# Half-row steps in the MLP phase of a spectral adaLN block's forward and backward pass

## The chip, the cores and the metric

The kernel runs on one core of a Trainium2 chip. The metric is device time in microseconds of one execution. Before the change the median of three runs is 533.21 us (532.02 to 536.06). Engines are named as in the profile: PE multiplies matrices (PEld loads its weights), DVE and ACT work on rows in SBUF and PSUM, SP issues the DMAs, POOL is hardly used here.

## The reference

S = 2048 rows, D = 512, F = 1792; all inputs are bf16. `c` and `w_mod` give six modulation rows, of which `gb`, `cb` and `ga` matter here. The outputs are the result of this block and its gradients for every input.

```
def A(x, w_r, w_i):                      # spectral filter
    X = rfft2(x) * (w_r + 1j * w_i)
    return irfft2(X)
def B(x, w1, b1, w2, b2):                # MLP, squared relu
    r = relu(x @ w1 + b1)
    return (r * r) @ w2 + b2
sa, ca, ga, sb, cb, gb = (silu(c) @ w_mod).reshape(6, D)
x1  = x  + ga * A(layernorm(x) * (1 + ca) + sa)
out = x1 + gb * B(layernorm(x1) * (1 + cb) + sb)
grads = vjp(out)(grad_out)
```

## The kernel before

The Fourier transforms are matmuls with constant matrices. The rows stand in 16 tiles of 128 rows, and the MLP phase takes them in four blocks of four tiles (512 rows); F is cut into 14 slices of 128. A number in brackets is the block.

Ahead of the MLP phase, PE computes gaT = (grad_out * 2gb) @ w2T, transposed, for all blocks: 224 matmuls of 512 columns (L601), that are given a late priority, so that they fill the gaps of the spectral stages. The MLP phase then has these stages for block b:

- `stage_g`: the last two spectral steps of each row tile (psT, L332, to Tsb on ACT; psY, L339, to y on ACT), then x1 and its layernorm on DVE, which gives n2rows.
- `stage_t`: 16 PE transposes of n2rows (L711) into h2T, evacuated by DVE and ACT in turn.
- `stage_h`: 14 slices of h (L732), relu on ACT (r, L733), then on DVE gh = r * gaT in place (L735) and h = r * r (L737); both are also written to DRAM.
- `stage_o`: for each row tile one matmul of b2 (L792) and 14 of h and w2 (L794), then out0 and gp = gb * o on DVE.
- `stage_gn`: for each row tile 14 matmuls of gh and w1T (L766), then on ACT and DVE cb, jk and the gradient row gx1, which is written to DRAM. For blocks 2 and 3 the first backward spectral step of that row (`spec_f1_row`, L232 to L239) follows late.
- `colsums` (L661): column sums on PE, delayed by two row tiles.

w1T is loaded by a transposing DMA after the last gaT matmul has freed its place, behind w2 and ahead of b2row on SP. It is then scaled by 1 + cb (L673) and has a mean added (L674, nmean). nmean comes from 56 one-column matmuls of w1 and the row 1 + cb (L668).

The first backward spectral step of the rows of blocks 0 and 1 (eight row tiles) needs the place UT that is only free in block 2; their gradient rows are loaded again from DRAM in pairs (L825), multiplied by ga on DVE (L826) and taken by PE in one block between `stage_h(2)` and `stage_o(2)`.

The program is written in stages in Python, but a scheduler with priorities sets the order on each engine: it takes an instruction that is ready, by its own costs, in the order of the program. Every engine then works in order. Tiles of a pool have a given number of buffers (`bufs`), and a new tile waits for the last use of the one it takes the place of.

Of the kernel before, what the change touches and what calls it, by code (L numbers as in the profile page):

```python
# [10 lines left out]
ALU = mybir.AluOpType  # L11
# [313 lines left out]
def spec_g23(tc, K, CS, t, tpool, psT_pool, psY_pool):  # L325

    nc = tc.nc
    ps = psT_pool.tile([P, D], FP32, name="psT")
# [7 lines left out]
    psY = psY_pool.tile([P, D], FP32, name="psY")  # L336
# [3 lines left out]
    return psY  # L340

# [65 lines left out]
def kernel(  # L407
# [174 lines left out]
    cb1b = constp.tile([P, 4], BF16, name="cb1b")  # L582
    nc.vector.tensor_copy(cb1b, mcol[:, CB1_C])
# [70 lines left out]
    with tc.tile_pool(name="psR", bufs=1, space=PSUM) as psR, tc.tile_pool(name="psO", bufs=2, space=PSUM) as psO_pool, \  # L654
# [10 lines left out]
        psr = psR.tile([P, NFC], FP32, name="pst2")  # L665
        for fc in range(NFC):
            for dc in range(4):
                nc.tensor.matmul(psr[:, fc:fc + 1], lhsT=w1[:, dc, fc * P:(fc + 1) * P], rhs=cb1b[:, dc:dc + 1],  # L668
                                 start=(dc == 0), stop=(dc == 3))
        nmean = wp.tile([P, NFC], FP32, name="nmean")  # L670
        nc.vector.tensor_scalar(nmean, psr, -1.0 / D, None, op0=ALU.mult)
        for fc in range(NFC):
            nc.vector.tensor_tensor(w1T[:, fc, :], w1T[:, fc, :], modb[:, CB1_B, :], op=ALU.mult)  # L673
            nc.vector.tensor_scalar(w1T[:, fc, :], w1T[:, fc, :], nmean[:, fc:fc + 1], None, op0=ALU.add)  # L674
# [4 lines left out]

        def stage_g(b):  # L680
            n2b[b] = rows.tile([P, TB, D], BF16, name="n2rows")
            x1b[b] = rows.tile([P, TB, D], BF16, name="x1")
            yb[b] = rows.tile([P, TB, D], BF16, name="y")
            nc.sync.dma_start(x1b[b], x_view[:, TB * b:TB * b + TB, :])
            for j in range(0, TB, 2):
                t = TB * b + j
                x1, y = x1b[b][:, j:j + 2, :], yb[b][:, j:j + 2, :]
                for i in range(2):
                    psY = spec_g23(tc, K, CS, t + i, rows, psR, psR)
                    nc.scalar.copy(out=y[:, i, :], in_=psY)  # L690
# [11 lines left out]
            nc.sync.dma_start(n2_dram[:, TB * b:TB * b + TB, :], n2b[b])  # L702

        def stage_t(b):
            n2rows = n2b[b]
            hb = rows.tile([P, 4, SB], BF16, name="h2T")
            h2T[b] = hb
            for dc in range(4):
                pst = psR.tile([P, TB, P], BF16, name="pst2")
                for j in range(TB):  # L710
                    nc.tensor.transpose(pst[:, j, :], n2rows[:, j, dc * P:(dc + 1) * P], K["ident"])  # L711
                src = pst.rearrange("p j q -> p (j q)")
                if dc % 2 == 0:
                    nc.vector.tensor_scalar(hb[:, dc, :], src, mcol[:, CB1_C, dc:dc + 1], mcol[:, SB_C, dc:dc + 1], op0=ALU.mult, op1=ALU.add)
# [399 lines left out]
```

## Time and profile before

| what | before |
|---|---|
| median of three runs | 533.21 us |
| the profiled execution | 533.43 us |
| its span | 531.6 us |
| granted PE clock, mean | 0.957 |
| PE busy | 450.7 us (85%) |
| DVE busy | 358.0 us (67%) |
| ACT busy | 239.7 us (45%) |

All times in the tables of stretches count from the start of the span. Ahead of 91 us lie the forward spectral steps, from 91 to 139 us the rest of gaT with the first two blocks' last spectral steps, from 139 to 335 us the four blocks of the MLP phase, and behind it the weight gradients and the rest of the backward spectral steps. In a timeline a row's start and length are given, and in square brackets how long its engine sat idle before it and which instruction ended that. Matmuls are pipelined, so that the lengths of neighbouring groups overlap; the distance of two starts is the better measure of what a group costs.

### The profile page before, as it was taken

The page shows a single profiled execution, that of the slowest core. Times are in us where ns is not written, and L with a number is a line of the kernel's source. Part 1 is how long each engine was busy: PE and PEld are TensorE (multiplying, and loading weights), DVE is VectorE, ACT ScalarE, POOL GpSimd, SP SyncE. Part 2 cuts the span into 40 slices and gives each one's busy share as a digit, 9 for nine tenths or more (in the row PEclk, how much of TensorE's full clock was granted, in tenths as well). Part 3 has the DMA queues.
Part 4 walks back from the last instruction along what each step waited for, and adds up shares of the span by engine and source line. Part 5 has one row for each costly group of instructions (what it writes and reads, how often), then busy time and mean ns, then how long its engine had stood idle before and what let it go on. Part 6 is the DMA issues. An engine that isn't in the chain of part 4 may idle for free.

```text
span 531.6 us, 7352 instructions
## 1 busy us (share of the span) xinstructions
PE 450.7 (85%) x2527; PEld 226.8 (43%) x2563; DVE 358.0 (67%) x849; ACT 239.7 (45%) x415; POOL 12.4 (2%) x56
## 2 busy tenths in 40 slices
PE   0868998899898999979599999866985999869995
PEld 0434465554343444434344434443442465424442
DVE  5878998294386670496647745267787667459976
ACT  3456865473453161345342722562312247626524
POOL 4111000000000000000000000000000000000000
PEclk9969999899999999999989999997899799979999
DMA  8954879420493298199511979575556619988997
GB/s 282 217 161 99 333 211 292 173 81 39 146 302 127 79 251 184 41 213 309 170 59 44 266 225 197 158 249 145 118 150 220 154 53 276 212 241 242 271 248 242
DMA packets 148062, 99.40 MB, mean 187 GB/s; under 512 B 93362, under 2 KB 134840, under 8 KB 147384
## 3 DMA queue, kind: packets, MB, share of 16 engines
q1 hardware_dynamic: 148024, 98.93, 68.0%
q8 instruction: 20, 0.33, 0.3%
q14 instruction: 18, 0.15, 0.1%
HBM read 37.26 MB, written 39.61 MB: 145 GB/s over the span
## 4 chain that ended last, share of the span: by engine, by line
PE 49%; DMA 17%; DVE 16%; SPq 11%; issue 3%; ACT 3%; DVEq 0%; ACTq 0%
PE og L794 9%; PE mm L732 7%; PE og L766 6%; PE mm L601 6%; PE mm L972 5%; PE mm L895 4%; SPq L494 3%; DMA w1T<-in_B_w_dram 3%; SPq L471 3%; DMA w1s<-in_B_w_dram 3%; PE psG L301 2%; PE psY L339 2%; PE psT L332 2%; DMA n_sb<-n_dram 2%; DMA gb<-in_grad_out_dram 2%
## 5 line engine op out<-in xcount | busy, mean ns | idle before, releaser
L895 PE MATMUL mm<-gab,n_sb 128*128 128x448 bf16 x256 | 56.0, 380 | 5.4 <-DVE gjk L903 5.4
L601 PE MATMUL mm<-gT,w2T 128*128 128x512 bf16 x213 | 53.8, 384 | 3.4 <-DVE gab L604 1.9
L732 PE MATMUL mm<-h2T,w 128*128 128x512 bf16 x219 | 52.9, 378 | 1.7 <-ACT h2T L716 0.9
L794 PE MATMUL og<-w,h 128*128 128x512 bf16 x218 | 52.0, 381 | 2.7 <-DVE h L737 2.4
L972 PE MATMUL mm<-g_sb,hn 128*128 128x512 bf16 x217 | 51.4, 384 | 0.5 <-issue 0.3
L766 PE MATMUL og<-w1T,gab 128*128 128x512 bf16 x218 | 49.7, 379 | 0.3
L733 ACT ACTIVATE r<-mm,b1col 128x512 bf16<-128x512 f32 x56 | 38.1, 687 | 20.1 <-PE mm L732 10.7
L895 PEld LDWEIGHTS <-n_sb 128*128 128x128 bf16 x256 | 26.5, 104 | 34.9 <-issue 15.7
L732 PEld LDWEIGHTS <-w 128*128 128x128 bf16 x224 | 21.3, 97 | 29.1 <-issue 7.9
L794 PEld LDWEIGHTS <-h 128*128 128x128 bf16 x224 | 20.7, 98 | 28.4 <-DVE h L737 3.9
L766 PEld LDWEIGHTS <-gab 128*128 128x128 bf16 x224 | 21.7, 98 | 26.0 <-issue 0.8
L601 PEld LDWEIGHTS <-w2T 128*128 128x128 bf16 x224 | 21.7, 98 | 25.9 <-issue 6.2
L972 PEld LDWEIGHTS <-hn 128*128 128x128 bf16 x224 | 21.2, 98 | 26.1 <-issue 3.8
L604 DVE CAST gab<-mm 128x512 bf16<-128x512 f32 x28 | 19.2, 687 | 18.5 <-PE mm L601 13.8
L770 DVE SCALAR_TENSOR_TENSOR jk<-cb,onef,n2rows 128x512 bf16<-128x512 bf16 x16 | 12.0, 749 | 27.8 <-ACT cb L767 27.8
L735 DVE TENSOR_TENSOR gab<-r,gab 128x1024 bf16<-128x1024 bf16 x28 | 19.3, 690 | 10.4 <-ACT r L733 10.4
L767 ACT ACTIVATE cb<-og,inv 128x512 bf16<-128x512 f32 x16 | 11.0, 688 | 33.4 <-PE og L766 33.4
L606 ACT CAST gab<-mm 128x512 bf16<-128x512 f32 x28 | 16.4, 587 | 20.7 <-PE mm L601 20.6
L335 ACT ACTIVATE Tsb<-psT 128x512 bf16<-128x512 f32 x32 | 18.3, 598 | 14.7 <-PE psT L332 14.6
L901 DVE SCALAR_TENSOR_TENSOR gw<-mm,mcol,gtmp 128x448 bf16<-128x448 f32 x16 | 10.9, 682 | 18.5 <-PE mm L895 17.5
L795 ACT CAST o<-og 128x512 bf16<-128x512 f32 x16 | 9.2, 588 | 30.4 <-PE og L794 27.5
L339 PE MATMUL psY<-Tsb,TAT 128*128 128x256 bf16 x128 | 18.8, 277 | 1.8 <-ACT y L690 1.5
(272 smaller groups left out, 791.4 us busy)
## 6 DMA issues: line engine op xcount, KB each, us to landing
gh_dram<-gab SPq DMA_DIRECT2D x28, 256.0 KB, 3.3
h_dram<-h SPq DMA_DIRECT2D x28, 256.0 KB, 3.1
w<-in_B_w_dram SPq DMA_DIRECT2D x2, 1792.0 KB, 8.0
wm<-in_w_mod_dram SPq DMA_DIRECT2D x3, 1024.0 KB, 8.2
wmc<-in_w_mod_dram SPq DMA_DIRECT2D x12, 256.0 KB
out_dram<-gwm SPq DMA_DIRECT2D x12, 256.0 KB, 3.9
xs_dram<-Xs SPq DMA_DIRECT2D x8, 258.0 KB, 3.3
Xb<-xs_dram SPq DMA_DIRECT2D x8, 258.0 KB, 3.0
```

Of the source, the lines that this page charges most:

```text
L335: nc.scalar.activation(Tsb, ps, AF.Copy, scale=EF_S)
L339: nc.tensor.matmul(psY[:, H * s:H * s + H], lhsT=K["TAT"][:, s * e], rhs=Tsb[:, H * e:H * e + H], start=(e == 0), stop=(e == 1))
L601: nc.tensor.matmul(ps, lhsT=w2T[:, dc, fc * P:(fc + 1) * P], rhs=gT[b][:, dc, :], start=(dc == 0), stop=(dc == 3))
L604: nc.vector.tensor_copy(out=gaT[b][:, fc, :], in_=ps)
L606: nc.scalar.copy(out=gaT[b][:, fc, :], in_=ps)
L732: nc.tensor.matmul(ps, lhsT=w1[:, dc, (fc + i) * P:(fc + i + 1) * P], rhs=h2T[b][:, dc, :], start=(dc == 0), stop=(dc == 3))
L733: nc.scalar.activation(r[:, i, :], ps, AF.Relu, bias=b1col[:, fc + i:fc + i + 1])
L735: nc.vector.tensor_tensor(gh, r, gh, op=ALU.mult)
L766: nc.tensor.matmul(ps, lhsT=gaT[b][:, fc, (j + i) * P:(j + i + 1) * P], rhs=w1T[:, fc, :], start=(fc == 0), stop=(fc == NFC - 1))
L794: nc.tensor.matmul(ps, lhsT=hT[b, fc][:, (j + i) * P:(j + i + 1) * P], rhs=w2[:, fc, :], start=False, stop=(fc == NFC - 1))
L895: nc.tensor.matmul(ps[:, 0:W4], lhsT=n2_sb[:, t, dc * P:(dc + 1) * P], rhs=ghn[t // 4][:, t % 4, fs], start=(t == 0), stop=(t == NT - 1))
L972: nc.tensor.matmul(ps, lhsT=hns[fc][:, t, :], rhs=g_sb[:, t, :], start=(t == 0), stop=(t == NT - 1))
```

## The change

Four things change.

(a) The 56 matmuls of L668 are gone. w1T is scaled by a SCALAR_TENSOR_TENSOR that also sums its row into nmean (L687 after); after all 14, nmean is scaled (L689) and added (L691).

(b) The stages return lists of steps, and `merge` deals them between each other: the steps of `stage_g(b+1)` and the transposing DMAs of the gh of block b-1 between the half rows (seven matmuls) of `stage_o(b)`, the transposes of `stage_t(b+1)` between the half rows of `stage_gn(b)`. The eight reloaded rows (`f1_again`, L865 and L866) go from the block ahead of `stage_o(2)` to between the half rows of `stage_gn(3)`. Their place is a buffer of `gx1` (two, shared with the gradient rows), no longer of `o`.

(c) x1 and grad_out rows (gb) are loaded by `load_rows` at the start of `stage_h` one block ahead, gb with two buffers instead of one; h2T has one buffer instead of two.

(d) In `stage_h`, h is computed and written ahead of gh.

```
-            for dc in range(4):
-                nc.tensor.matmul(psr[:, fc:fc + 1], lhsT=w1[:, dc, fc * P:(fc + 1) * P], rhs=cb1b[:, dc:dc + 1],
-                                 start=(dc == 0), stop=(dc == 3))
-        nc.vector.tensor_scalar(nmean, psr, -1.0 / D, None, op0=ALU.mult)
+            nc.vector.scalar_tensor_tensor(out=w1T[:, fc, :], in0=w1T[:, fc, :], scalar=K["onef"], in1=modb[:, CB1_B, :], op0=ALU.mult, op1=ALU.mult,
+                                           accum_out=nmean[:, fc:fc + 1])
+        nc.vector.tensor_scalar(nmean, nmean, -1.0 / D, None, op0=ALU.mult)
         for fc in range(NFC):
-            nc.vector.tensor_tensor(w1T[:, fc, :], w1T[:, fc, :], modb[:, CB1_B, :], op=ALU.mult)
             nc.vector.tensor_scalar(w1T[:, fc, :], w1T[:, fc, :], nmean[:, fc:fc + 1], None, op0=ALU.add)
...
+def merge(main, *fills):
+    fill = [f for fl in fills for f in fl]
+    k = 0
+    for i, m in enumerate(main):
+        m()
+        while k < len(fill) and k * len(main) < (i + 1) * len(fill):
+            fill[k]()
+            k += 1
...
+        def load_rows(b):
+            if b < NB:
+                x1b[b] = rows.tile([P, TB, D], BF16, name="x1")
+                nc.sync.dma_start(x1b[b], x_view[:, TB * b:TB * b + TB, :])
+            if b > 0:
+                gbt[b - 1] = rows.tile([P, TB, D], BF16, name="gb")
+                nc.sync.dma_start(gbt[b - 1], g_view[:, TB * (b - 1):TB * b, :])
...
+        def f1_again(UT):
+            gxl = {}
+            def one(t):
+                if t % 2 == 0:
+                    gxl[0] = rows.tile([P, 2, D], BF16, name="gx1")
+                    nc.sync.dma_start(gxl[0], gx1_dram[:, t:t + 2, :])
+                    nc.vector.tensor_tensor(gxl[0], gxl[0], modb[:, GA_B, None, :].broadcast_to([P, 2, D]), op=ALU.mult)
+                spec_f1_row(tc, K, gxl[0][:, t % 2, :], t, UT, psR, ("psT", "psY")[t % 2])
+            return [lambda t=t: one(t) for t in range(2 * TB)]
...
+        for b in range(NB):
+            stage_h(b)
+            parts = [lambda fc=fc: ghn_part(b - 1, fc) for fc in range(0, NFC, 2)] if b > 0 else []
+            if b < NB - 1:
+                merge(stage_o(b), [x for p in zip(stage_g(b + 1), parts + [lambda: None] * 8) for x in p])
+                if b == NB - 2:
+                    UT = utcs.tile([P, 4, 16, NT, 8], BF16, name="utcs")
+                merge(stage_gn(b, UT), [lambda: None] * 2 + stage_t(b + 1))
+            else:
...
+                merge(stage_gn(b, UT), [x for p in zip(f1_again(UT), parts + [lambda: None]) for x in p])
+                merge(stage_o(b))
```

What stands on an engine is decided by the scheduler, so three places follow as the two programs have them. The first is DVE at the end of `stage_h(0)`, where w1T is prepared. Before (the last rows of the preparation, six more pairs of L673 and L674 stand ahead):

```order
L673 TENSOR_TENSOR w1T<-w1T,modb 128x512 x2
L674 TENSOR_SCALAR w1T<-w1T,nmean 128x512 x2
L737 TENSOR_TENSOR h<-r 128x1024
L735 TENSOR_TENSOR gab<-r,gab 128x1024
L737 TENSOR_TENSOR h<-r 128x1024
L714 TENSOR_SCALAR h2T<-pst_1908,mcol 128x512
L735 TENSOR_TENSOR gab<-r,gab 128x1024
L737 TENSOR_TENSOR h<-r 128x1024
```

The same place after the change (gab is gh, L773 is h, L847 belongs to `stage_o(0)`):

```order
L773 TENSOR_TENSOR h<-r 128x1024
L777 TENSOR_TENSOR gab<-r,gab 128x1024
L749 TENSOR_SCALAR h2T<-pst_1950,mcol 128x512
L773 TENSOR_TENSOR h<-r 128x1024
L687 SCALAR_TENSOR_TENSOR w1T,nmean<-w1T,onef,modb 128x512 x14
L777 TENSOR_TENSOR gab<-r,gab 128x1024
L689 TENSOR_SCALAR nmean<-nmean 128x14
L847 TENSOR_TENSOR gp<-gb,o 128x1024
L691 TENSOR_SCALAR w1T<-w1T,nmean 128x512 x14
```

All h of the block now stand ahead of the preparation, whose two passes are apart. On PE, the 16 transposes of block 0, and four of block 1, have moved from between the first matmuls of `stage_h(0)` to among the last gaT matmuls.

The second place is ACT from the end of `stage_h(2)` to `stage_o(2)`. Before (r is of `stage_h`, y and Tsb of the spectral steps of block 3, utcs of the reloaded rows, o of `stage_o`):

```order
L733 ACTIVATE r<-mm,b1col 128x512 x14
L690 CAST y<-psY 128x512 x2
L335 ACTIVATE Tsb<-psT 128x512
L690 CAST y<-psY 128x512 x2
L239 CAST utcs<-psY 128x64x8
L239 CAST utcs<-psT 128x64x8
L349 ACTIVATE inv_70<-l_mv,eps 128x2
L239 CAST utcs<-psY 128x64x8
L349 ACTIVATE inv_70<-l_mv,eps 128x2
L239 CAST utcs<-psY 128x64x8
L795 CAST o<-og 128x512 x2
```

After:

```order
L771 ACTIVATE r<-mm,b1col 128x512 x2
L717 CAST y<-psY 128x512
L335 ACTIVATE Tsb<-psT 128x512
L771 ACTIVATE r<-mm,b1col 128x512 x8
L371 ACTIVATE inv_70<-l_mv,eps 128x2
L771 ACTIVATE r<-mm,b1col 128x512 x4
L842 CAST o<-og 128x512 x3
L717 CAST y<-psY 128x512
L842 CAST o<-og 128x512
L717 CAST y<-psY 128x512
L806 ACTIVATE cb<-og,inv_70 128x512
```

The spectral steps of block 3 now stand within `stage_h(2)` and `stage_o(2)`, and the reloaded rows are no longer there; PE has the transposes of block 3 between the rows of `stage_gn(2)`, where before they stood in and behind that block. The same steps of block 2 stand where they stood, within and behind `stage_gn(1)`.

The third place is DVE in `stage_gn(3)`. Before:

```order
L770 SCALAR_TENSOR_TENSOR jk,rb<-cb,onef,n2rows 128x512
L771 TENSOR_SCALAR rb<-rb 128x1
L770 SCALAR_TENSOR_TENSOR jk,rb<-cb,onef,n2rows 128x512
L771 TENSOR_SCALAR rb<-rb 128x1
L772 SCALAR_TENSOR_TENSOR gx_3199<-n2rows,rb,gb 128x512 x2
L770 SCALAR_TENSOR_TENSOR jk,rb<-cb,onef,n2rows 128x512
```

After (L866 is the multiply of a reloaded pair):

```order
L811 SCALAR_TENSOR_TENSOR gx_3072<-n2rows,rb,gb 128x512
L866 TENSOR_TENSOR gx_3121<-gx_3121,modb 128x1024
L809 SCALAR_TENSOR_TENSOR jk,rb<-cb,onef,n2rows 128x512
L810 TENSOR_SCALAR rb<-rb 128x1
L811 SCALAR_TENSOR_TENSOR gx_3072<-n2rows,rb,gb 128x512
L815 TENSOR_TENSOR gx_3072<-gx_3072,cb 128x1024
L818 TENSOR_TENSOR cb<-gx_3072,modb 128x1024
L820 TENSOR_TENSOR y<-gx_3072,y 128x1024
L866 TENSOR_TENSOR gx_3171<-gx_3171,modb 128x1024
L809 SCALAR_TENSOR_TENSOR jk,rb<-cb,onef,n2rows 128x512
```

The multiplies of three reloaded pairs stand among the rows of `stage_gn(3)`. All four reloads take the same buffer of gx1 one after the other, so that the DMA of each waits for the matmuls of the pair before it.

More of the change, by code (lines that the diff above doesn't have):

```diff
@@ L335, in spec_g23, with spec_g3 @@
     nc.scalar.activation(Tsb, ps, AF.Copy, scale=EF_S)
[L336 removed]
+    return Tsb
+def spec_g3(tc, K, Tsb, pool):
+    nc = tc.nc
+    psY = pool.tile([P, D], FP32, name="psY")
+    H = D // 2
     for s in range(2):
```

165 lines of the change are left out of this document (78 added, 87 removed).

## The prediction

> **What bounds the kernel now.** I read the page first: the busy shares, and the shares of the chain that ended last.
>
> ```profile
> PE 450.7 (85%) x2527; PEld 226.8 (43%) x2563; DVE 358.0 (67%) x849; ACT 239.7 (45%) x415; POOL 12.4 (2%) x56
> PE 49%; DMA 17%; DVE 16%; SPq 11%; issue 3%; ACT 3%; DVEq 0%; ACTq 0%
> ```
>
> PE is busy for 85% of the span but makes only 49% of the chain, so a good part of the time goes through work that PE waits for. To find where, I cut the MLP phase into stretches. The columns are the stretch, its length, the busy time and instructions of PE, PEld, DVE, ACT and POOL, the granted PE clock, the DMA share and GB/s.
>
> ```profile
> 97.00:139.00 42.00, 40.36 (x212) 21.32 (x215) 25.29 (x53) 21.69 (x40) 0.00 (x0) 0.96 0.16 55
> 139.00:187.00 48.00, 42.91 (x213) 18.92 (x217) 30.03 (x67) 18.54 (x28) 0.00 (x0) 1.00 0.61 181
> 187.00:237.00 50.00, 46.12 (x231) 20.82 (x235) 29.14 (x62) 21.34 (x36) 0.00 (x0) 1.00 0.70 172
> 237.00:291.00 54.00, 47.39 (x240) 22.75 (x242) 34.23 (x67) 22.13 (x38) 0.00 (x0) 0.94 0.48 153
> 291.00:335.00 44.00, 42.68 (x208) 18.92 (x210) 25.09 (x47) 17.54 (x28) 0.14 (x2) 1.00 0.87 210
> ```
>
> PE is the bound in all of them: in the second to fifth row it lacks 5.1, 3.9, 6.6 and 1.3 us of busy time. Two rows stand out: 139 to 187 (block 0) and 237 to 291 (block 2), the latter also with a clock of 0.94. These, and the one matmul group that the change removes, I read in the timeline of PE (start, length, line, instruction, idle time before it and its releaser). First the removed group:
>
> ```profile
> 95.45 1.57 PE L668 MATMUL pst<-cb1b,w 128*128 128x1 bf16 x56 [3.66 <-DMA w<-in_B_w_dram]
> ```
>
> Then block 0, from the last gaT matmul to the first h of block 1:
>
> ```profile
> 133.69 5.28 PE L601 MATMUL mm<-gT,w2T 128*128 128x512 bf16 x22
> 139.24 0.38 PE L711 MATMUL pst<-ident,n2rows 128*128 128x128 bf16 x4 [0.26 <-DVE nmean L671]
> 140.26 0.38 PE L711 MATMUL pst<-ident,n2rows 128*128 128x128 bf16 x4 [0.64 <-DVE h2T L714]
> 140.48 0.59 PE L732 MATMUL mm<-h2T,w 128*128 128x512 bf16 x2
> ...
> 148.59 7.43 PE L732 MATMUL mm<-h2T,w 128*128 128x512 bf16 x32 [0.18 <-ACT r L733]
> 155.85 0.39 PE L711 MATMUL pst<-ident,n2rows 128*128 128x128 bf16 x4
> ...
> 163.12 1.04 PE L794 MATMUL og<-w,h 128*128 128x512 bf16 x4 [2.36 <-DVE h L737]
> ...
> 170.83 0.38 PE L792 MATMUL og<-b2row,ones_sq 1*128 1x512 bf16 x1
> ...
> 174.18 12.25 PE L766 MATMUL og<-w1T,gab 128*128 128x512 bf16 x55
> ...
> 186.91 1.47 PE L732 MATMUL mm<-h2T,w 128*128 128x512 bf16 x6
> ```
>
> PE runs dry at the first transposes, and later for 2.36 us at the last slices of h. gaT ends at 133.69 + 5.28 = 138.97, which I call E, and block 1 starts at 186.91 = E + 47.9. Then block 2, between its h and its rows of h*w2, where the spectral steps of block 3 (L339), the reloaded rows (L232, operand o) and the transposes (L711) stand in a row:
>
> ```profile
> 255.36 0.60 PE L339 MATMUL psY<-Tsb,TAT 128*128 128x256 bf16 x4 [0.68 <-ACT y L690]
> ...
> 259.93 0.27 PE L232 MATMUL psT<-TA,o 128*128 128x256 bf16 x1 [1.43 <-DVE utcs L237]
> ...
> 263.55 0.61 PE L711 MATMUL pst<-ident,n2rows 128*128 128x128 bf16 x2 [1.43 <-DVE n2rows L701]
> 265.13 0.39 PE L232 MATMUL psT<-TA,o 128*128 128x256 bf16 x1 [0.97 <-DVE o L826]
> ...
> 268.96 0.60 PE L792 MATMUL og<-b2row,ones_sq 1*128 1x512 bf16 x1
> ...
> 291.10 3.11 PE L732 MATMUL mm<-h2T,w 128*128 128x512 bf16 x13
> ```
>
> Each step here waits for another engine, and nothing else is queued on PE that could go ahead. The same stretch as a window:
>
> ```profile
> 254.69:268.96 14.27, 8.27 (x48) 5.22 (x49) 11.20 (x26) 6.90 (x14) 0.00 (x0) 0.82 0.35 116
> ```
>
> PE is busy 8.27 of 14.27 us, and at a clock of 0.82, though no single wait is over 1.43 us.
>
> **Part 1, up to the end of gaT.** L668 waited 3.66 us for the load of w1 and took 1.57 us; gaT matmuls, which wait for nothing there, take its place: -5.2. The 20 transposes that now stand among the gaT matmuls cost PE (from the start of 140.26 to that of 140.48, four in 0.22) 20 x 0.055 = +1.1, and leave the next part. Sum -4.1. Bounds: -5.2 if they fit into waits that are there, and -2.2 if n2rows, which DVE makes just before, comes late for two waits like the one of 0.97 at 265.13.
>
> **Part 2, from E to block 1.** Here I build the time forward, since the waits change places. 32 matmuls of h go from 148.59 to 155.85, 0.227 each, so 56 end at E + 12.7, as the transposes are done by then and, with all h ahead of w1T on DVE, the wait of 2.36 is gone. What is late next is a DMA: `stage_o(0)` begins with b2row. SP's rows, and the transposing load from the chain of waits:
>
> ```profile
> 139.44 12.54 SPq L646 DMA_TRANSPOSE w1T<-in_B_w_dram  x1
> 152.03 0.42 SPq L648 DMA_DIRECT2D b2row<-in_B_b_dram  x1
> ```
>
> ```profile
> 139.44 14.54 DMA w1T<-in_B_w_dram
> ```
>
> SP is held for 12.54 us by the issue of w1T and gives out b2row at 152.03. Its landing has no row of its own; the nearest is that of the DRAM tile of gradient rows, for 256 KB:
>
> ```profile
> DMA to landing us min/median/max: 2.1/3.7/5.7
> ```
>
> I take its least, 2.1 us, for 1 KB: 154.1 or E + 15.2, a new wait of 2.5 us. SP waits for the same gaT matmul before and after, so this moves with E. A row of h*w2 takes 174.18 - 170.83 = 3.35, four 13.4: E + 28.6. Then `stage_gn(0)`, by the row at 174.18 12.2 us, the 12 transposes left 0.7 and the column sums 186.91 - 186.43 = 0.5, gives block 1 at E + 42.0 if w1T is ready. That is decided on DVE:
>
> ```profile
> L770 DVE SCALAR_TENSOR_TENSOR jk<-cb,onef,n2rows 128x512 bf16<-128x512 bf16 x16 | 12.0, 749 | 27.8 <-ACT cb L767 27.8
> ```
>
> ```profile
> L673 DVE TENSOR_TENSOR w1T<-w1T,modb 128x512 bf16<-128x512 bf16 x14 | 5.3, 422 | 0.2 <-DMA w1T<-in_B_w_dram 0.2
> L674 DVE TENSOR_SCALAR w1T<-w1T,nmean 128x512 bf16<-128x512 bf16 x14 | 4.3, 351 | 0.0
> ```
>
> w1T lands at 139.44 + 14.54 = E + 15.0. The old scaling took 0.42 an instruction, or 5.3 us for all; the new one I price by jk, the same operation with a sum in the same shape, 0.749: 14 make 10.5, E + 25.5. Three instructions stand between, at most 0.75 each, so the additions begin by E + 27.7 and end 4.3 us later, E + 32.0. The first is needed at 28.6, the last at 28.6 + 13/14 of a row of 3.05 = 31.4: +0.6. Block 1 starts at E + 42.6, against 47.9: **-5.3**. gab of the last pair now waits behind the 14 scalings, but is needed in `stage_gn(0)` alone, as late as those. Bounds: -5.9 with w1T in time, and -1.7 with b2row at the largest landing, 5.7.
>
> **Part 3, blocks 1 and 2 up to the h of block 3.** For block 2's spectral steps the order is unchanged, so `stage_gn(1)` and what follows stay as they are: 0. The earlier loads of x1 and gb take waits from DVE that PE does not see there: 0. In block 2 the row of 14.27 us breaks up. What stays on PE are 16 matmuls of psY at 0.109 (half of one of 512 columns) and four transposes, 1.9 in all, now between rows; 12.4 go. Of the waits I let one stay, the 1.43 for n2rows: the second pair's layernorm is still made on DVE while `stage_gn(2)` starts, and the transposes stand in order ahead of its later rows. **-11.0**. Bounds: -12.4 without this wait, and -3.5 if every wait comes back in the new place and only the reloaded rows leave.
>
> **Part 4, block 3.** The eight reloaded rows come back here. Two rows of this kind, when nothing waits, take
>
> ```profile
> 295.26:296.14 0.88, 0.88 (x10) 0.78 (x9) 0.88 (x2) 0.57 (x2) 0.00 (x0) 1.00 1.30 250
> ```
>
> 0.88 us, four pairs 3.5. Their loads are no longer hidden: each waits for the previous pair's matmuls, since they share one buffer. The first load is issued in `stage_gn(2)` and is in time. Between pairs PE has, by the order, 18 matmuls and six column sums (4.4 us at 0.217, 12.2/56), then 15 (3.3), then 17 and four of 256 columns (4.1): 11.8 of cover. Against it stands a landing L, 0.7 for the multiply (1024 columns, at two of the 0.35 that L674 takes) and 0.3 that I allow for the signals. L is the last number of these rows, of the same 256 KB from the same tile:
>
> ```profile
> gxl<-gx_dram SPq DMA_DIRECT2D x8, 256.0 KB, 4.0
> o<-gx_dram SPq DMA_DIRECT2D x4, 256.0 KB, 5.3
> ```
>
> With 4.0 the three waits are 0.6 + 1.7 + 0.9 = 3.2, with 5.3 they are 7.1. I take the middle, 5.1, as the last stretch of the table has a DMA share of 0.87, but the writes of h end before. The sum is 3.5 + 5.1 = **+8.6**. Bounds: +3.5 if all is covered, +11.8 at L = 5.7 (8.3 of waits).
>
> [...]
>
> **The sum.** -4.1 - 5.3 - 11.0 + 8.6 = -11.8. The profiled execution took 533.43 us (0.22 above the median; its span of 531.6 and 1.8 around it), so 521.6. What follows the MLP phase keeps its order and moves along.
>
> **Rivals.** First, *the reload chain eats the gain*. DVE works in order, and in `stage_gn(3)` jk, which frees the rows for PE, stands behind a multiply that waits for a load. The three waits come to 3 x (L + 1) - 11.8; the time is within 1% of before from L = 6.9 on, and all is lost at L = 8.6. The largest landing in the trace, 5.7, gives 524.8, and speaks against more. Second, *the waits only move*: block 3's steps stand between rows now, but its y, layernorm and transposes still need ACT and DVE in turn, and in-order PE waits inside `stage_o(2)`. With part 3 at -3.5 the time is 529.1. The window of `stage_gn(1)` and its follow-up, where psY and transposes of block 2 do stand among rows, speaks half for it, PE being busy 20.63 of 24 us:
>
> ```profile
> 212.00:236.00 24.00, 20.63 (x119) 10.34 (x120) 16.48 (x41) 9.92 (x17) 0.00 (x0) 1.00 0.45 110
> ```
>
> Third, and *slower*: the clock. The window at 254.69 had 0.82 with many short waits. If the cutting up of rows brought that clock to all four pairs of `stage_o` and `stage_gn`, 13.4 + 12.2 or about 26 us each, 104 us would take 1/0.82 - 1 = 22% longer, +22.8, and the kernel 544 us. It breaks even at a clock of 0.90, and is 1% slower from 0.86. Against it: the window of 212 to 236 has just such a mix, and 1.00.
>
> [...]
>
> **How the numbers follow.** I give the forecast, 516 to 525 us, 0.53; better still, by covered reloads, 0.13; the reload chain at its bound, 524.8 to 527.9, 0.11; the waits that only move, and a slower chain, 527.9 to 538.5, 0.17; the clock 0.06. A measurement of this kernel can't tell less than about 1%, 527.9 or 538.5, from no change. So faster is 0.77, same 0.17, slower 0.06. The parts' better ends give -5.2 - 5.9 - 12.4 + 3.5 = -20.0, or 513; the worse ends together are past the other side, and 530 takes in the second rival. Range 513 to 530, which leaves out 0.04 below and some 0.15 above.
>
> **What would show it.** Right: no idle time of 3.66 near 95 us; gaT ends near 134.9; PE's wait ahead of the first row of h*w2 is about 2.5 us, released by the DMA of b2row; DVE has 14 scalings of about 0.75 behind it; between the h of block 2 and of block 3 there is no window under a clock of 0.95; `stage_gn(3)` has three waits for DVE's L866, and DVE there for the DMA of gx1, 5 us in all; the MLP phase ends some 12 us earlier. Wrong: L866's waits over 12 us in sum, a wait for n2rows inside `stage_gn(2)` of several us, or a granted clock under 0.95 in the merged rows.

## The result, and the profile after

The changed kernel takes 513.49 us (median of four runs, 512.27 to 516.24), the kernel before 532.71 in the same comparison: a ratio of 0.963, 95% interval 0.957 to 0.970. Run again beside other kernels it took 513.17 against 530.18, 0.971 (0.965 to 0.977). The forecast was 521.6, with a range of 513 to 530: faster, as forecast, but by 17 to 19 us where 12 were expected.

The page of the profiled execution (516.24 us, span 514.5), busy shares and chain:

```profile
PE 453.1 (88%) x2507; PEld 226.1 (44%) x2507; DVE 363.1 (71%) x862; ACT 239.5 (47%) x415; POOL 12.5 (2%) x56
PE 56%; DVE 17%; DMA 11%; SPq 8%; ACT 5%; issue 3%; DVEq 0%; ACTq 0%
```

PE does nearly the same work in less time, and its share of the chain has gone from 49% to 56%. The stretches of the MLP phase, cut at the end of gaT and at the first h of each block (length, busy time and count of PE, PEld, DVE, ACT and POOL, granted clock, DMA share, GB/s):

```profile
97.00:135.60 38.60, 37.45 (x219) 19.95 (x218) 25.02 (x53) 21.95 (x40) 0.00 (x0) 1.00 0.26 88
135.60:176.80 41.20, 40.49 (x193) 17.30 (x191) 33.12 (x79) 16.57 (x25) 0.00 (x0) 1.00 0.70 211
176.80:223.90 47.10, 45.31 (x228) 20.24 (x226) 31.48 (x65) 19.86 (x33) 0.00 (x0) 1.00 0.70 184
223.90:268.70 44.80, 43.56 (x230) 19.56 (x227) 28.51 (x58) 20.73 (x34) 0.00 (x0) 1.00 0.59 165
268.70:320.50 51.80, 48.82 (x237) 22.66 (x234) 29.27 (x53) 20.00 (x33) 0.14 (x2) 0.93 0.70 183
```

Block 0 (second row) lacks 0.7 us of PE instead of 5.1, block 2 (fourth row) 1.2 us, and its clock is 1.00 instead of 0.94. Block 3 (last row) is what has become longer, and it has a clock of 0.93. The timeline of PE up to block 1:

```profile
92.42 0.60 PE L621 MATMUL mm<-gT,w2T 128*128 128x512 bf16 x2
...
93.06 2.83 PE L621 MATMUL mm<-gT,w2T 128*128 128x512 bf16 x12
...
120.31 15.41 PE L621 MATMUL mm<-gT,w2T 128*128 128x512 bf16 x68
135.63 12.88 PE L770 MATMUL mm<-h2T,w 128*128 128x512 bf16 x56
149.23 0.38 PE L746 MATMUL pst<-ident,n2rows 128*128 128x128 bf16 x4 [0.71 <-DVE h2T L749]
...
149.97 0.39 PE L788 MATMUL og<-b2row,ones_sq 1*128 1x512 bf16 x1
...
176.83 1.47 PE L770 MATMUL mm<-h2T,w 128*128 128x512 bf16 x6
```

There is no wait near 95 us, the h of block 0 follow gaT at once (E is now 135.63), 56 in one piece, the first row of h*w2 starts at 149.97 = E + 14.3 behind a wait of 0.71 for the transposes of block 1, and block 1 starts at E + 41.2. The columns of the next table are times between such starts: from the first gaT matmul behind 89 us (90.99 before, 92.42 after) to the first h of block 2; from there to the first h of block 3; from there to the first matmul of the spectral step that follows the MLP phase; and from there to the end of the span.

| kernel | median us | to block 2 | block 2 | block 3 | sum | behind it |
|---|---|---|---|---|---|---|
| before | 532.71 | 141.6 | 58.5 | 43.8 | 243.9 | 196.7 |
| after | 513.49 | 131.5 | 44.8 | 52.4 | 228.6 | 193.4 |
| after, again | 513.17 | 131.5 | 44.8 | 50.7 | 227.0 | 194.3 |
| new w1T alone | 526.83 | 133.4 | 57.4 | 48.1 | 238.8 | 192.1 |
| new w1T and h first | 523.30 | 131.3 | 56.3 | 46.7 | 234.2 | 194.8 |
| after, old w1T | 523.70 | 142.8 | 44.8 | 49.4 | 237.0 | 192.9 |
| after, not merged | 513.86 | 132.2 | 44.9 | 49.1 | 226.1 | 194.9 |
| before, rows later | 529.33 | 144.0 | 48.9 | 52.2 | 245.1 | 193.3 |
| before, transposes later | 535.23 | 150.2 | 55.1 | 45.4 | 250.8 | 195.0 |
| before, both moves | 531.55 | 150.7 | 46.9 | 50.6 | 248.2 | 195.1 |
| after, early loads | 510.62 | 131.3 | 44.5 | 47.9 | 223.7 | 195.6 |
| after, early loads in o | 510.72 | 131.5 | 44.9 | 46.1 | 222.6 | 196.0 |
| after, both (first) | 516.40 | 126.7 | 50.1 | 53.4 | 230.2 | 192.0 |
| after, both (second) | 506.83 | 127.1 | 46.5 | 46.1 | 219.7 | 191.8 |

The runs of before had medians of 530.2 to 532.7 in the different comparisons, and single runs scatter by some 5 us to either side, so differences under 1% are read from the stretches, which repeat better: the two profiles of the changed kernel agree within 0.1 us in the first two. In the kernels that keep the one-column matmuls the first stretch also holds their wait for w1, which was 3.50 to 5.32 us in these profiles, and the slow clock behind it (0.50 from 96.62 to 100.03 us before), so that it repeats less well there.

### The profile page after: what moved, and what is told of

Its sections match the earlier page's. It is cut to its first block, busy times and chain, and to the rows that moved or that the text cites. A ratio compares the mean times of both kernels' runs of the same rounds, so it can differ in the third digit from the quotient of the medians.

```text
span 514.5 us, 7304 instructions
## 1 busy us (share of the span) xinstructions
PE 453.1 (88%) x2507; PEld 226.1 (44%) x2507; DVE 363.1 (71%) x862; ACT 239.5 (47%) x415; POOL 12.5 (2%) x56
## 4 chain that ended last, share of the span: by engine, by line
PE 56%; DVE 17%; DMA 11%; SPq 8%; ACT 5%; issue 3%; DVEq 0%; ACTq 0%
PE og L790 16%; PE mm L770 9%; PE mm L621 7%; PE mm L948 6%; PE psG L301 3%; SPq L516 3%; DMA w1s<-in_B_w_dram 2%; PE psY L346 2%; PE psT L332 2%; PE psB L274 2%; SPq L518 2%; PE psC L261 2%; DVE jk L1092 2%; DMA n<-n_dram 1%; DVE gm_junk L423 1%
## 5 line engine op out<-in xcount | busy, mean ns | idle before, releaser
L948 PE MATMUL mm<-gab,n_sb 128*128 128x448 bf16 x256 | 54.4, 372 | 5.7 <-DVE gjk L956 5.7
L621 PE MATMUL mm<-gT,w2T 128*128 128x512 bf16 x224 | 55.4, 380 | 1.9 <-DVE gab L624 1.6
L790 PE MATMUL og<-w1T,gab 128*128 128x512 bf16 x224 | 54.2, 391 | 0.0
L773 DVE TENSOR_TENSOR h<-r 128x1024 bf16<-128x1024 bf16 x28 | 19.3, 690 | 15.0 <-ACT r L771 14.9
L847 DVE TENSOR_TENSOR gp<-gb,o 128x1024 bf16<-128x1024 bf16 x8 | 5.5, 689 | 28.7 <-ACT o L842 28.7
L952 ACT ACTIVATE gtmp<-gb1bc,mcol 128x448 f32<-128x448 bf16 x16 | 10.3, 665 | 22.8 <-DVE gw L954 22.7
```

The lines of the kernel that those rows point to most:

```text
L621: nc.tensor.matmul(ps, lhsT=w2T[:, dc, fc * P:(fc + 1) * P], rhs=gT[b][:, dc, :], start=(dc == 0), stop=(dc == 3))
L773: nc.vector.tensor_tensor(h2, r, r, op=ALU.mult)
L790: nc.tensor.matmul(ps, lhsT=lhs(fc), rhs=rhs[:, fc, :], start=(fc == 0 and init is None), stop=(fc == NFC - 1))
L948: nc.tensor.matmul(ps[:, 0:W4], lhsT=n2_sb[:, t, dc * P:(dc + 1) * P], rhs=ghn[t // 4][:, t % 4, fs], start=(t == 0), stop=(t == NT - 1))
```

## The experiments

**The changed kernel again.**

> The changed kernel once more, unaltered, beside the others. Theory A (the gain is made up to the last column sums of the MLP phase, and the 3.2 us by which the part behind them was shorter in the profiled execution is scatter between executions): 513 to 515 us, and the part from the last column sums to the end of the span lies anywhere from 192 to 198 us. Rival (the change also shortens what follows the MLP phase): that part stays at 193 to 195 us.

513.17 us. What lies behind the MLP phase took 194.3 us here and, over all kernels of the table, 191.8 to 196.7, without regard to the change: kernels with the order of before had 192.1 to 195.1. The 196.7 of the profile of before is the longest of all. So the 3.2 us that the two profiles differ there are not from the change, as far as one profile of each can say.

**The new preparation of w1T alone**, put into the kernel before:

```
-            nc.tensor.matmul(psr[:, fc:fc + 1], ... rhs=cb1b[:, dc:dc + 1] ...)
-        nc.vector.tensor_scalar(nmean, psr, -1.0 / D, None, op0=ALU.mult)
+            nc.vector.scalar_tensor_tensor(out=w1T[:, fc, :], ... accum_out=nmean[:, fc:fc + 1])
+        nc.vector.tensor_scalar(nmean, nmean, -1.0 / D, None, op0=ALU.mult)
```

> The kernel before with only the new preparation of w1T (no one-column matmuls, scaling with a sum). Theory A: the removed matmuls give 5.2 and the transposes of block 0 move up among the gaT matmuls, as their PSUM buffer is no longer held by nmean's matmuls; but in this order two pairs of h stand behind the 14 scalings of 0.67, so that PE's wait for h in block 0 grows from 2.4 to about 5 us. Net -3 us, 530. Rival (the new preparation is worth its share of parts 1 and 2 by itself): -8 to -9 us, 524.

526.83 us, 0.993 (0.989 to 0.998): the theory's 3 us. The stretch to block 2 is 8.2 us shorter and block 2 1.1, and 4.3 us are lost again in block 3, where PE once waits 3.59 us for a row of cb. In its timeline of PE two of the predicted waits can be seen:

```profile
149.27 0.38 PE L787 MATMUL og<-b2row,ones_sq 1*128 1x512 bf16 x1 [0.66 <-DMA b2row<-in_B_b_dram]
...
159.57 1.04 PE L789 MATMUL og<-w,h 128*128 128x512 bf16 x4 [2.19 <-DVE h L732]
```

The wait for b2row is there, 0.66 us, and with the last h behind 14 scalings PE still waits 2.19 us for it.

**The same with h ahead of gh**, which the change has too:

```
-                gh = gaT[b][:, fc:fc + 2, :]
-                nc.vector.tensor_tensor(gh, r, gh, op=ALU.mult)
                 h2 = hring.tile([P, 2, SB], BF16, name="h")
                 nc.vector.tensor_tensor(h2, r, r, op=ALU.mult)
+                gh = gaT[b][:, fc:fc + 2, :]
+                nc.vector.tensor_tensor(gh, r, gh, op=ALU.mult)
```

> The kernel before with the new preparation of w1T and with h ahead of gh in every block. Up to the h of block 2 the time from the first gaT matmul behind 89 us is 141.6 us before, 133.4 with the new preparation alone, 131.5 after. Theory: the rest is h ahead of gh, by which the last h stands ahead of the 14 scalings on DVE and PE's wait of 2.2 us in block 0 goes: 131 to 132, the time 523. Rival (it is the order of the stages and the earlier loads): stays at 133 to 134.

523.30 us, 0.990 (0.981 to 0.999), and 131.3 us to block 2. The timeline of PE:

```profile
137.63 14.51 PE L727 MATMUL mm<-h2T,w 128*128 128x512 bf16 x63
152.90 0.39 PE L787 MATMUL og<-b2row,ones_sq 1*128 1x512 bf16 x1 [0.76 <-DMA b2row<-in_B_b_dram]
```

63 matmuls of h in one piece from the end of gaT, then 0.76 us for b2row, and no wait for h. These two edits make all of the gain up to block 2 (131.5 in the changed kernel) without any new order of stages.

**The changed kernel with the old w1T.**

> The changed kernel with the old preparation of w1T (one-column matmuls back, scaling without a sum). Theory A: the wait near 93 us and the matmuls come back (+5), the transposes of block 0 go back behind gaT (+2.3) and h waits behind w1T again (+2.4): 523 us. Rival (the order of the stages alone makes the gain in block 0, and the one-column matmuls cost only themselves): +5 us, 518.5.

523.70 us, 0.990 (0.982 to 0.997), and 142.8 us to block 2: what the removed matmuls were worth comes back in full, 11.3 us, although h stands ahead of gh here; in block 0 PE waits 2.41 us for h again. The one-column matmuls cost much more than themselves: their result used the PSUM buffer of the transposes (both are called pst2) until DVE had read nmean behind the last gaT, so that no transpose could go ahead (in the kernel before, the first transpose at 139.24 is released by nmean).

**The changed kernel, not merged.**

```
-                merge(stage_o(b), [x for p in zip(stage_g(b + 1), parts + [lambda: None] * 8) for x in p])
+                merge(stage_g(b + 1))
+                merge(stage_o(b), parts)
...
-                merge(stage_gn(b, UT), [lambda: None] * 2 + stage_t(b + 1))
+                merge(stage_gn(b, UT))
+                merge(stage_t(b + 1))
```

> The changed kernel with the lists of steps one after the other: spectral steps of the next block, then the rows of h*w2, then the rows of gh*w1T, then the transposes; the reloaded rows stay in block 3 and the loads stay early. Theory A (the block ahead of the rows of h*w2 in block 2 is gone already because the reloaded rows left it, and the scheduler by itself puts block 3's spectral steps among h; what merging adds is the transposes, some 2 us for each of three blocks): 519 us. Rival (merging itself makes the gain of 11 us in block 2): 524 us or more.

513.86 us, 0.974 (0.965 to 0.982). Both expectations fell: without merging in blocks 0 to 2 nothing is lost (the reloaded rows still stand between the half rows of block 3). The windows of its blocks 2 and 3:

```profile
221.90:266.90 45.00, 43.50 (x223) 19.53 (x221) 30.60 (x62) 19.51 (x32) 0.00 (x0) 1.00 0.59 173
266.90:315.90 49.00, 47.29 (x250) 22.15 (x247) 28.72 (x51) 21.65 (x35) 0.14 (x2) 1.00 0.75 189
```

44.9 us for block 2, as in the changed kernel, and 49.1 for block 3, less than there. So it is not the steps between half rows that made the gain; the order of whole stages, out of which the scheduler then picks, was enough. This is where my reading of the change was wrong.

**The reloaded rows moved, alone**, in the kernel before:

```
-        for t in range(2 * TB):
...
         stage_o(2)
         stage_gn(2, UT)
         stage_h(3)
...
+        for t in range(2 * TB):
...
         stage_gn(3, UT)
```

> The kernel before with one edit: the eight reloaded rows stand ahead of the rows of gh*w1T of block 3 instead of ahead of the rows of h*w2 of block 2. The stretch from the first gaT matmul behind 89 us to the first matmul of the spectral step that follows the MLP phase is 243.9 us before and 227 to 229 after. Theory B (formed on the run without merging, whose stretch was 226.1: the gain in block 2 is the reloaded rows leaving the place where they barred PE, and the scheduler then spreads the rest by itself): the h of block 3 begins 46 to 48 us after the h of block 2 instead of 58.5, block 3 grows by 5 to 8, the stretch is 238 to 240 us. Rival (the place of the transposes, behind the rows of gh*w1T, makes that gain): the stretch stays over 242 us.

529.33 us, 0.998 (0.994 to 1.002), the stretch 245.1 us: neither. Block 2 is 9.6 us shorter, and block 3 8.4 us longer: the move by itself changes the place of the time and hardly its sum. The 2.4 us more up to block 2 lie ahead of the first h, where the wait for w1 was 5.00 us in this profile instead of 3.66; the edit does not reach there. What block 2 still has above the changed kernel stands at its end, ahead of the h of block 3, in the timeline of PE:

```profile
277.31 0.23 PE L711 MATMUL pst<-ident,n2rows 128*128 128x128 bf16 x1 [0.79 <-DVE n2rows L701]
...
281.20 0.61 PE L711 MATMUL pst<-ident,n2rows 128*128 128x128 bf16 x2 [3.18 <-DVE n2rows L701]
282.57 0.58 PE L711 MATMUL pst<-ident,n2rows 128*128 128x128 bf16 x4 [0.77 <-DVE h2T L714]
```

The layernorm of block 3 comes late here, and the transposes wait 4.7 us in all.

**The transposes moved, alone.**

```
-        stage_t(1)
         stage_o(0)
         stage_gn(0)
+        stage_t(1)
```

and so for each block.

> The kernel before with one edit: the transposes of the next block stand behind the rows of gh*w1T instead of behind h; the reloaded rows stay where they are. Theory B: with the reloaded rows still ahead of the rows of h*w2 some of the waits stay, but the transposes and the layernorm no longer bar PE; the stretch is 239 to 241 us, the h of block 3 begins 52 to 54 us after the h of block 2. Rival (the place of the transposes makes the gain in block 2): the h of block 3 begins 48 us after, the stretch is 235 us.

535.23 us, 1.005 (1.001 to 1.009), the stretch 250.8 us: slower, if anything. It gains 3.4 us in block 2 but loses 8.6 up to there. Of these, 2.5 lie ahead of the first h, behind a wait for w1 of 4.71 us, and 6.1 in blocks 0 and 1, where PE once waits 2.56 us for y ahead of the column sums of block 1, with slow matmuls behind it (two of h take 1.06 us at 240.39, against 0.59 at 140.48 in the kernel before). The rest of the 6.1 was not followed up.

**Both moves**, in the kernel before, nothing merged:

> The kernel before with two edits together: the reloaded rows in block 3 and the transposes behind the rows of gh*w1T, nothing merged. Each alone gave nothing (the stretch 245.1 and 250.8 against 243.9). Theory (the two only pay together, since either one left in place still bars PE in block 2): from the h of block 2 to the end of the MLP phase 94 to 96 us instead of 102, as in the changed kernel, the stretch 238, the time 526. Rival (it needs the spectral steps of the next block behind h, too, as the changed kernel has them): over 100 us there, no gain.

531.55 us, 1.003 (0.998 to 1.008): no gain in time, as the rival said, but not for its reason. The profile is of the longest of the ten executions (536.48 us), so its lengths are read with care; where a step stands does not depend on that. The spectral steps of block 3 stand among the h of block 2, as they already do with the transposes moved alone:

```profile
245.99 0.60 PE L339 MATMUL psY<-Tsb,TAT 128*128 128x256 bf16 x4
```

Blocks 2 and 3 take 46.9 and 50.6 us, together 97.5 instead of 102.3, near the 95.5 to 97.2 of the changed kernel and not over 100. The gain there is lost up to block 2, which takes 9.1 us longer: 3.3 ahead of the first h, behind a wait of 5.32 us for w1, and 5.8 in blocks 0 and 1, as with the transposes moved alone. So the transposes' move puts the spectral steps early, and with the reloaded rows gone as well blocks 2 and 3 come within about 2 us of the changed kernel in this one profile, nearly as the theory had it. The changed kernel also has the spectral steps behind h, the earlier loads and one buffer of h2T; which of these keeps its blocks 0 and 1 from paying was not tried one by one.

**The reloads early, in places of their own** (the changed kernel; the loads are issued ahead of `stage_h(3)`):

```
-                    gxl[0] = rows.tile([P, 2, D], BF16, name="gx1")
-                    nc.sync.dma_start(gxl[0], gx1_dram[:, t:t + 2, :])
+            for k, nm in enumerate(("x1", "n2rows")):
+                gxl[k] = rows.tile([P, TB, D], BF16, name=nm)
+                nc.sync.dma_start(gxl[k], gx1_dram[:, TB * k:TB * k + TB, :])
```

First what the changed kernel has in block 3. PE, then DVE, then SP, and the group of the DMA:

```profile
286.20 0.27 PE L233 MATMUL psY<-TA,gx 128*128 128x256 bf16 x1
...
293.95 0.40 PE L232 MATMUL psT<-TA,gx 128*128 128x256 bf16 x1 [2.94 <-DVE gx L866]
...
295.63 5.55 PE L790 MATMUL og<-w1T,gab 128*128 128x512 bf16 x15
```

```profile
293.20 0.69 DVE L866 TENSOR_TENSOR gx<-gx,modb 128x1024 bf16<-128x1024 bf16 x1 [4.67 <-DMA gx<-gx_dram]
```

```profile
288.61 0.67 SPq L887 DMA_DIRECT2D Cdb<-Cd_dram  x1
289.37 6.82 SPq L865 DMA_DIRECT2D gx<-gx_dram  x2
```

```profile
gx<-gx_dram SPq DMA_DIRECT2D x4, 256.0 KB, 2.8
```

The first pair's matmuls end at about 286.5, but SP gives out the next load at 289.37, as the writes of h and gh and the load of Cdb stand ahead of it. (The row of SP merges two loads, the second one issued at 295.87.) Only two of the four loads have a landing on record, and 2.8 is their median; of this one it is known that DVE starts on it 3.8 us after the start of its issue (293.20). DVE waits 4.67 and PE 2.94 us. And behind the wait PE is slow: 15 matmuls start over 5.4 us, 0.36 each, where 0.217 is usual. The window behind it:

```profile
294.00:302.00 8.00, 8.00 (x32) 4.08 (x33) 5.25 (x11) 1.86 (x3) 0.00 (x0) 0.63 0.19 66
```

> The changed kernel with the eight reloaded rows loaded into two places of their own (a buffer of x1 and one of n2rows, both free by then), issued ahead of the h of block 3 instead of one pair after the other through one buffer of gx1. Theory A, with what the trace after showed (one wait of 2.5 to 2.9 us for a reload, and behind it some 15 matmuls at 0.36 instead of 0.22 us, at a granted clock of 0.67): both go, and no window of block 3 is under 0.95; the part from the h of block 3 to the end of the MLP phase is 46 to 47.5 us instead of 50.7 to 52.4; the kernel 4 to 5 us faster, 509. Rival (the clock is unrelated to the wait, and the reloads would be late in the other places too as SP gives them out late): 1 us at most.

510.62 us, 0.960 (0.949 to 0.971). Block 3 took 47.9 us, a little over what was expected, and as one window it has a clock of 1.00:

```profile
268.00:316.00 48.00, 46.04 (x242) 21.93 (x240) 28.13 (x52) 20.66 (x34) 0.14 (x2) 1.00 0.80 192
```

The theory's part with the reloads and the clock holds. A new wait was made, though: the multiply of the rows in n2rows stands ahead of h on DVE, and PE waited 1.73 us for r behind that:

```profile
280.08 3.73 PE L770 MATMUL mm<-h2T,w 128*128 128x512 bf16 x16 [1.73 <-ACT r L771]
```

**The same with the buffers of o** in place of n2rows:

```
-            for k, nm in enumerate(("x1", "n2rows")):
...
+            for t, nm, n in ((0, "x1", TB), (TB, "o", 2), (TB + 2, "o", 2)):
+                tl = rows.tile([P, n, D], BF16, name=nm)
+                nc.sync.dma_start(tl, gx1_dram[:, t:t + n, :])
```

> The kernel as above but without the early column sums: only the reloaded rows in x1 and o, loaded ahead of the h of block 3. Theory: as with the first early loads, whose block 3 took 47.9 us, but without the wait of 1.7 us for r (there the multiply of the rows in n2rows stood ahead of h on DVE and waited for its load): block 3 takes 46 to 47 us, the stretch 222 to 223, the time 509. Rival (that wait comes from the writes of h and gh on SP): block 3 stays at 47.9.

510.72 us, 0.967 (0.960 to 0.974); block 3 46.1 us, the stretch 222.6: as expected, the wait for r is gone. Against block 3 of the changed kernel in its two profiles (50.7 and 52.4), loading early into places of their own is worth 4.6 to 6.3 us. How much of that is the buffer and how much the place in SP's queue, these runs do not separate.

**Early loads and early column sums**, first version (the loads in x1 and n2rows, and one flush of the delayed column sums):

```
                 merge(stage_gn(b, UT), [lambda: None] * 2 + stage_t(b + 1))
+                if b == 0:
+                    late.flush()
```

> The kernel with early loads, and in addition the delayed column sums of block 0 are let go at the end of that block, so that a buffer of y is free and the spectral steps of block 2 can stand in block 1 as written. Theory: what kept them in and behind the rows of gh*w1T of block 1 was the buffer of y; with it free, the h of block 2 begins about 44 us after that of block 1 instead of 47, without waits for Tsb. 506 us, the stretch 219 to 220. Rival (PE fills that time with other work anyway): as the kernel with early loads alone, 509.

516.40 us, 0.971 (0.962 to 0.979): worse than either expectation. To block 2 it gains 4.8 us, so the buffer of y was what held block 2's spectral steps back. But block 2 and block 3 give back 5.3 and 1.0 us (against the first profile of the changed kernel; 5.5 us in block 3 against early loads alone). DVE, SP and PE there:

```profile
278.39 0.69 DVE L870 TENSOR_TENSOR n2rows<-n2rows,modb 128x1024 bf16<-128x1024 bf16 x1 [6.41 <-DMA n2rows<-gx_dram]
```

```profile
263.22 6.63 SPq L760 DMA_TRANSPOSE gab<-gh_dram  x5
...
272.32 0.52 SPq L864 DMA_DIRECT2D n2rows<-gx_dram  x1
```

```profile
266.64 0.55 PE L746 MATMUL pst<-ident,n2rows 128*128 128x128 bf16 x2 [2.59 <-DVE n2rows L734]
...
281.74 1.18 PE L770 MATMUL mm<-h2T,w 128*128 128x512 bf16 x3 [3.76 <-ACT r L771]
```

SP issues the transposing loads of gh for 6.63 us ahead of the second reload; that lands late, DVE waits 6.41 us for it with h of block 3 queued behind, and PE 3.76 us. The other wait, 2.59 us, is for the layernorm of block 3, which still came late.

**The second version**: the buffers of x1 and o, and a flush behind blocks 0 and 1:

```
+                if b < NB - 2:
+                    late.flush()
```

> The changed kernel with three edits: the reloaded rows go into a buffer of x1 and the two of o (free from the end of the rows of h*w2 of block 2 to those of block 3), all loads issued ahead of the h of block 3; and the delayed column sums of blocks 0 and 1 are let go at the end of each block, so that a buffer of y is free and the spectral steps of blocks 2 and 3 both stand among the rows of h*w2 as written. Theory (PE's remaining waits are those at buffers held too long: y by the late column sums, gx1 by the reloads; the run with both early sums and early loads lost what it had gained because its second load stood behind the transposing DMAs on SP, DVE behind it, and because block 3's y was still held): from the h of block 1 to that of block 2 42 to 43 us instead of 47.1, to that of block 3 43 to 45, to the end of the MLP phase 46 to 47.5; the stretch 216 to 219 us, the time 502 to 506. Rival (DVE, 9.9 of 10 us busy around the layernorm of block 3 in that run, is the bound as soon as PE's waits go): stretch 223 or more, 510.

506.83 us, 0.960 (0.951 to 0.968), and the stretch 219.7 us, a little over what was expected. It is the fastest of all kernels here: 23.5 us under the kernel before (530.32 in this comparison), and 6.3 us under the changed one by the medians, 7.3 to 8.9 by the stretch. Its blocks 1, 2 and 3:

```profile
175.57:218.06 42.49, 42.06 (x212) 18.36 (x211) 29.63 (x60) 19.37 (x32) 0.00 (x0) 1.00 0.68 192
218.06:264.60 46.54, 45.69 (x241) 21.20 (x240) 33.06 (x66) 21.37 (x36) 0.00 (x0) 1.00 0.67 187
264.60:310.65 46.05, 46.03 (x243) 21.92 (x241) 26.97 (x49) 20.63 (x34) 0.14 (x2) 1.00 0.75 189
```

PE lacks 0.4, 0.9 and 0.0 us. From 150 to 310 us no wait of PE is over 0.6 us. DVE is busy for 59 to 71%, so that the rival does not hold. Block 1 is as expected; block 2, at 46.5 us, is longer than the expected 43 to 45 and than in the changed kernel, with 45.7 us of work on PE. What is left in this phase is PE's own work.

## Why the prediction was right, and where its sizes were off

The sign and the main places were right: faster, by PE's waits at the one-column matmuls, at the start of block 0, and in block 2, paid back in part by the reloaded rows. The sum of -11.8 stands against -15.3 in the same stretch of the profiled executions (-16.9 in the repeated one). Their spans differ by 17.1 us; 3.2 us less lie behind the MLP phase and 1.4 us more ahead of the first gaT matmul, which the other runs do not tie to the change. The time, 513.49, lies half a microsecond inside the range's better end, in the band to which I gave 0.13, and not for the reason named with it: the reloads were not covered. (Also, by the prediction's own sum the reload chain comes within 1% of before from L = 6.7 on, not 6.9.)

Part 1, -4.1: the size is right. From the first gaT matmul to E it is 43.2 us (92.42 to 135.63) after 48.0 (90.99 to 138.97), -4.8. The reason given was incomplete, though. I priced the wait and the matmuls, and took the transposes' move for a thing of the order; the PSUM buffer that the two share made it a part of the removal. I also left out the clock. Behind the wait of 3.66 us the old kernel has a clock of 0.62 from 97 to 101 us, and the changed one 1.00 in its whole stretch up to the end of gaT; that is 1.5 us by an estimate (0.38 of 4 us). So that the sum came out near is in part luck.

Part 2, -5.3: -6.7 at the first h of block 1, of which 1.4 came back in block 1 (45.7 before, 47.1 after), in part since before PE had done six of block 1's matmuls within block 0, and now two. The two terms that I put in were both too large. SP:

```profile
136.18 11.17 SPq L666 DMA_TRANSPOSE w1T<-in_B_w_dram  x1
147.40 0.43 SPq L668 DMA_DIRECT2D b2row<-in_B_b_dram  x1
```

The issue of w1T took 11.17 instead of 12.54 us, and PE starts on the rows of h*w2 at E + 14.3 and not 15.2, behind the wait of 0.71 for h2T; no wait for b2row is left (0.66 and 0.76 us in two other kernels). The scalings:

```profile
L687 DVE SCALAR_TENSOR_TENSOR w1T<-w1T,onef,modb 128x512 bf16<-128x512 bf16 x14 | 9.5, 747 | 1.0 <-DMA gh_dram<-gab 1.0
L691 DVE TENSOR_SCALAR w1T<-w1T,nmean 128x512 bf16<-128x512 bf16 x14 | 3.8, 344 | 0.0
```

0.747 us each, as jk, but 9.5 us for 14, as each starts 0.67 after the one before: I had added durations that overlap. w1T is in time, and my +0.6 is not there.

Part 3, -11.0: -13.7 in block 2. The wait that I let stay, 1.43 us for n2rows, is 0.42:

```profile
252.67 0.60 PE L346 MATMUL psY<-Tsb,TAT 128*128 128x256 bf16 x4
...
257.64 0.27 PE L746 MATMUL pst<-ident,n2rows 128*128 128x128 bf16 x2
...
260.07 0.23 PE L746 MATMUL pst<-ident,n2rows 128*128 128x128 bf16 x1 [0.42 <-DVE n2rows L734]
...
268.69 1.47 PE L770 MATMUL mm<-h2T,w 128*128 128x512 bf16 x6
```

and the clock came back to 1.00, which I had counted only within the row of 14.27 us. The reason was wrong in one respect: I put the gain down to the steps standing between rows; without merging it is the same, 44.9 us. What makes the spectral steps of block 3 go early is the move of the transposes. Alone it gives nothing, as the reloaded rows then still stand among them; both moves together bring block 2 of the old kernel to 46.9 us, in one profile, though they lose the gain again up to block 2.

Part 4, +8.6: +8.6 in the profiled execution, +6.9 in the repeated one, but this is the right sum of wrong terms. I had three waits of 5.1 us from loads of 4.65 us. The two landings on record took 2.6 and 3.0, and only one wait was left, 2.94 or 2.54 us, because SP gave that load out 2.9 us after its place was free; besides the 3.5 us of the rows themselves, the rest is mostly the slow clock behind the wait. Both landings are under the rows of 4.0 and 5.3 that the prediction took its L from, while the load that PE waited for took up to 3.8 us from its issue to its use. The 0.3 us that I allowed for the signals is shown by no run; from the end of the multiply to PE's first matmul it was 0.06 us (293.89 to 293.95).

The rivals: the reload chain was real, and loading early is worth 4.6 to 6.3 us, but it was not long enough to eat the gain. That the waits only move did not happen in the changed kernel, but it is what came of the single moves. The clock stayed at 1.00 in all merged rows of blocks 0 to 2, so the rival that forecast slower did not come true there. In those of block 3 it fell to 0.93 over the block, which is one of the signs of being wrong that the prediction named; that came behind the one long wait, of 2.94 us.

## What to carry to other kernels

A small computation can cost more by the buffer that it holds than by its time: before pricing a removal, list who else uses its tiles. Where a scheduler picks the order, which stage stands ahead of which, and when buffers come free, decides; dealing steps by hand between half rows added nothing in blocks 0 to 2 here. A load that is issued in time by the program can still be late in its DMA queue: look at what the issuing engine has ahead of it, here 2.9 us of other issues.

## What the hardware showed that was not expected

Behind the longer waits of PE the clock was lower: 0.77 from 292.50 to 300.00 behind 2.54 us (the changed kernel again), 0.63 from 294 to 302 behind 2.94 us (the changed kernel), 0.77 from 311.70 to 319.00 behind 3.59 us (the new w1T alone). Below that the length of one wait did not tell: behind 2.36 us in block 0 before the clock was 1.00 from 163.12 to 170.83, and behind 2.05 us in the changed kernel with the old w1T 1.00 from 299 to 306; there, too, the four matmuls behind 2.41 us took 1.04 us, as the four behind 2.36 us before. But behind 2.11 us in block 3 of the kernel with the new w1T and h first it was 0.50 from 311.15 to 314.56. The same place in three runs: 2.94 us above, then the repeated run of the changed kernel, and the changed kernel with the old w1T:

```profile
292.49 0.28 PE L232 MATMUL psT<-TA,gx 128*128 128x256 bf16 x1 [2.54 <-DVE gx L866]
...
293.97 4.47 PE L790 MATMUL og<-w1T,gab 128*128 128x512 bf16 x15
```

```profile
301.87 0.28 PE L232 MATMUL psT<-TA,gx 128*128 128x256 bf16 x1 [2.05 <-DVE gx L871]
...
302.75 3.40 PE L795 MATMUL og<-w1T,gab 128*128 128x512 bf16 x15
```

The 15 matmuls behind the wait start over 5.4, 4.3 and 3.4 us (by the next row, or the length of the group), 0.36, 0.29 and 0.23 each. So the step from 2.05 to 2.94 us of wait cost 0.9 us of waiting and 2.0 us in these matmuls alone.

In the traces of the kernel before and of the changed one every piece of 3.41 us between 60 and 345 us, counted from 263.87 before and from 293.15 in the changed kernel, has a clock of either 1.00 or 0.50. It was 0.50 from 96.62 to 100.03 and from 263.87 to 270.69 before, and from 293.15 to 299.97, from 330.69 to 334.11 and from 337.52 to 340.93 in the changed kernel; the first of these three began within the wait of 2.94 us, which ended at 293.95. In pieces of this length, the places of the waits of 2.94, 2.05 and 2.11 us are, in this order:

```profile
289.74:293.15 3.41, 1.27 (x10) 0.31 (x4) 0.00 (x0) 0.48 (x1) 0.00 (x0) 1.00 0.75 227
293.15:296.56 3.41, 2.61 (x11) 1.57 (x12) 3.22 (x7) 1.17 (x2) 0.00 (x0) 0.50 0.00 0
```

```profile
297.68:301.09 3.41, 2.14 (x13) 0.52 (x11) 0.00 (x0) 0.69 (x1) 0.00 (x0) 1.00 0.70 224
301.09:304.50 3.41, 2.63 (x17) 1.60 (x18) 3.24 (x7) 1.07 (x2) 0.00 (x0) 1.00 0.10 30
```

```profile
307.74:311.15 3.41, 1.30 (x8) 0.66 (x8) 3.41 (x9) 0.69 (x1) 0.00 (x0) 1.00 0.13 50
311.15:314.56 3.41, 3.41 (x12) 1.53 (x11) 3.34 (x8) 0.58 (x1) 0.00 (x0) 0.50 1.10 129
```

The wait of 2.05 us is parted between two pieces in which PE is busy for 2.14 and 2.63 us; the one of 2.11 us falls into a single piece and leaves 1.30. In the traces of before and after, a clock of 0.50 followed all five full-speed pieces with PE busy for 1.37 us or less, and none with 1.75 or more. Around 264 us in the kernel before no wait is over 1.43 us, but PE is busy for only 1.34 us from 260.45 to 263.87, just ahead of the slow clock. These are counts of two traces; no run varied the waits alone.
